# Attention into an expert layer on one core: v kept on partitions 32 to 95, halo rows copied on chip, second buffers for raw k and q, and a new order list

## The chip, the cores and the metric

One core of a Trainium2 chip runs the whole kernel. The metric is the device time of one execution in microseconds (us); the median of several runs is compared. The engines are named as the profile names them: PE (TensorE matmuls), PEld (its weight loads), DVE (VectorE), ACT (ScalarE), POOL (GpSimd) and SP (SyncE). In this kernel POOL issues every load, and SP issues the stores.

## The reference

B = 4 batches, H = 8 heads, S = 768 rows, D = 64. Each query attends to the keys within 15 rows of it and to 24 summaries, one for each block of 32 keys (the maximum of k over the block, the mean of v). The result goes through an expert layer.

```python
k_sum = k.reshape(B, H, nb, 32, D).max(axis=3)
v_sum = v.reshape(B, H, nb, 32, D).mean(axis=3)
scores_l = where(abs(i - j) < 16, scale * q @ k.T, -1e9)
scores_s = scale * einsum('bhsd,bhnd->bhsn', q, k_sum) + log(32)
a = softmax(concatenate([scores_l, scores_s], -1))
x = (a @ concatenate([v, v_sum], 2)).transpose(0, 2, 1, 3).reshape(3072, 512)
h = x @ w_in                               # [512, 2048]
out = (h * clip(h + 3, 0, 6) / 6) @ w_out  # [2048, 512], float32
```

## The kernel before

**Tiles.** A batch has 12 tiles of 64 queries. A tile's keys are a window of 96 rows plus the 24 summaries, 120 in all (`KEYS`). Scores are computed with the keys on the partitions, so that one exponential serves 120 partitions, and `kaug` (k, transposed) and `vaug` hold, for each tile, its 96 window rows and the 24 summaries. The queries are shifted by 16 rows (`PAD`) against the keys, so that a window is 64 rows of its own plus 32 rows that belong to the next tile. In `vaug` the tile's own 64 rows lie on partitions 0 to 63, the 32 rows ahead on 64 to 95, the summaries on 96 to 119. `vaug` has two buffers; batch b uses b % 2.

**Loads.** `load_v` (L381) brings v, a pair of heads at a time, to partitions 0 to 63. The rows ahead come once more from HBM with `load_vhalo` (L388: one POOL DMA at L393, and a small SP DMA at L395) for batches 1 to 3, and are copied on chip by `halo` (L398) for batch 0. Batch 0's k and q are loaded in natural form and transposed by PE (`k_step` L440, `q_step` L482); those of batches 1 to 3 come "raw" (`load_raw` L362: k in four DMAs of 32 partitions, q in eight DMAs of 16 partitions) and are transposed in blocks of 32 by DVE (`turn` L584, with L588, L592 and the maxima of L605). The raw buffers `kraw` and `qraw` are single, so batch 2's raw loads wait for batch 1's transposes. `load_w` (L414) and `load_w2` (L420) bring the expert's weights in four chunks each.

**Work.** `scores` (L502) makes scores (L519), exponential (L527, ACT) and mask (L531, DVE) for a pair of heads and half a batch. `vsum_first` (L546) and `vsum` (L560) make the block means of v with an indicator matrix `ind` and spread them to the tiles. `values` (L613) multiplies with `vaug`, and `finish` normalises, transposes and leaves `x`. The expert layer runs over eight sub-batches of 384 rows: `f1` (L692) is the first product (L700: four matmuls into an `h` bank, the relu at L705 on ACT, the product `g` at L707 on DVE), `f2` (L711) the second: four chunks of four matmuls (L720), a copy out of the bank to `ot` (helper L432), a store. PSUM has two pairs of banks for S, three banks for h, and a single bank, o, for the second product, so a new group of L720 begins when the last one's copy is done.

**Order.** Every operation has a key, and the list `ORDER` names all of them in the order in which they are issued; `Plan.run` (L147) walks it. Each engine executes its own operations in that order. A tag is a letter and numbers: K, Q, V are loads (`K23` is group 3 of batch 2's k), H the halo loads, I and O the chunks of w_in and w_out, k and q the transposes of batch 0, w a `turn`, s scores, u block means, h a halo copy, v values, F and G the expert's first and second product (sub-batch, then group); `.0`, `.1` ... are the steps, and `:A` or `:D` puts a step on ACT or DVE. The planner's costs (`SLOW`, `KRAW`, `LAT`) only decide how many idle matmuls `keep` (L800) puts into PE's early pauses. Waits between engines are put in by the framework from what each operation reads and writes; nothing overtakes on an engine.

Of the kernel before, what the change touches and what calls it, by code (L numbers as in the profile page):

```python
# [15 lines left out]
D = 64  # L16
BLK = 32
# [4 lines left out]
VW = 66  # L22
# [7 lines left out]
c.0 K00.0 c.7 K01.0 c.10 c.11 c.12 c.13 c.9 c.1 Q000.0 K02.0 Q010.0 c.2 c.3 k00.0 k01.0 q010.0 k01.1 k01.4 k00.1 q010.1:A  # L30
k00.4 c.4 k00.3:A k01.2 s010.0 q030.0 q000.0 q000.1:A s030.0 s010.1 s010.2 q020.0 q020.1:A k00.2 q030.1:D k01.3:D k03.0
k03.1 k02.0 k02.1 V00.0 V01.0 c.6 V02.0 V03.0 I0.0 I1.0 Q001.0 s000.0 u00.0 s000.1 u01.0 k03.3:A k03.2 k02.2 u00.1:D u00.2:D
k03.4 u01.1:D s000.2 u01.2:A u00.3:D k02.4 h21.0:D k02.3:D u02.0 s020.0 s030.1 s020.1 s020.2 u03.0 h30.0:D h00.0:D h10.0:D
h01.0:D v00.0 v02.0 u03.1:D u03.2:D v00.2 u01.3:D v00.3 u02.1:A s030.2 h20.0:A u02.2:A Q011.0 I2.0 I3.0 O0.0 O1.0 O2.0 O3.0
K10.0 K11.0 K13.0 K12.0 v01.0 v01.2 v02.1 v00.1 v02.4 v00.4 v00.5 v02.2 v02.3 v02.5 v00.6 v01.1 v01.3 v01.4 v01.5 h31.0:A
v00.7:A u03.3:A q001.0 q011.0 q001.1:A q021.0 q021.1:A u02.3:D q011.1:D v01.6 v02.6 q031.0 s021.0 v01.7:A h11.0:D v02.7:D
c.5 c.8 s021.1 F00.0 F00.1 F00.2 F00.10 F00.3 F01.0 F01.1 s001.0 s001.1 s021.2 q031.1:D F00.4 F01.2 s001.2 F00.11 F00.12
s011.0 F00.13 F00.14 Q121.0 Q101.0 Q110.0 Q100.0 Q120.0 Q131.0 Q130.0 Q111.0 s011.1 s011.2 s031.0 F00.5 F00.6 F00.7 F01.9
F00.8 F00.9 F02.6 s031.1 F01.3 F02.7 F01.10 F01.4 s031.2 F02.8 v04.0 v03.0 F01.6 F01.11 F01.5 v03.1 v03.2 F01.7 F01.8 v04.1
F02.3 F02.4 F02.5 F02.9 v03.3 v03.4:A F02.10 v04.2 F00.15 F02.0 v05.0 v04.3 F00.16 F02.1 F02.11 F00.17 F02.2 v05.1 v05.2  # L40
F03.3 F03.9 F03.0 v04.4:A F03.4 v05.3 F03.1 F03.10 v05.4:A G01.0 F03.5 F03.11 F03.2 F03.6 F10.0 F03.7 F12.0 F03.8 F10.1
F10.3 F12.1 F10.2 F12.2 F10.6 F10.4 F10.9 F10.5 F10.7 F10.8 F11.0 F10.10 F10.11 F11.6 F11.1 F11.9 F11.2 F11.7 F11.8 F11.10
F11.11 F12.6 F12.7 F12.8 F12.9 F12.10 F12.11 w12.0 G01.1 F13.0 F13.1 w13.0 F13.2 w11.0 w13.3 w10.0 w12.3 G01.2 G01.3 F12.3
F13.9 G01.4:A G02.0 G02.1 G02.2 G02.3 F11.3 F13.10 w11.2:A F12.4 F12.5 G02.4:A w12.2:A F13.3 F11.4 F13.4 w10.2:A w13.2:A
w12.4 w11.3 w11.4 w11.1 w11.5:D G00.0 G00.1 s110.0 s110.1 s110.3 w12.1 w13.1 w12.5:D w13.5:A G00.2 G00.3 s120.0 s120.1
s120.3 w13.4 w10.1 F13.5 w10.3 F11.5 w10.4 w10.5:D F13.11 V10.0 V13.0 V11.0 V23.0 V12.0 H1.0 K20.0 K22.0 V20.0 K21.0 Q231.0
K23.0 Q220.0 V22.0 V21.0 Q200.0 Q221.0 Q201.0 Q211.0 Q210.0 Q230.0 s130.0 G00.4:A F13.6 G12.0 s130.3 s130.1 F13.7 G00.5
G01.5 H1.1 G02.5 s120.2 s110.2 s130.2 s100.0 s100.1 F13.8 s100.2 s110.4 s100.3 G12.1 u1.0 u1.1:A u1.3:A u1.5:A G12.2 G12.3
G12.4:A u1.4:D u1.2:D v10.0 s120.4 v10.1 v10.5 v10.6 v10.2 s100.4 u1.7:A u1.6:A u1.9:A G11.0 G11.1 v12.0 v10.3 v10.4:A
u1.8:A v12.1 v12.2 s130.4 G11.2 v10.7 v12.3 v10.8:D G11.3 v12.4:A v13.0 F20.0 F20.3 G11.4:A F20.1 F20.4 v13.5 v13.1 v13.2  # L50
v13.6 F20.9 v13.3 v15.0 F20.10 F20.2 F20.5 F20.11 v15.1 v15.2 F20.6 F21.0 F20.7 F20.8 F21.1 V30.0 V31.0 V32.0 V33.0 F21.2
w21.0 F21.6 G10.0 F21.7 v13.4:A F21.8 F21.3 v15.3 v13.7 F21.9 F22.3 F21.4 F21.5 w20.0 F22.0 G10.1 F21.10 F22.4 v15.4:A
F21.11 F22.1 F22.5 F22.9 F23.0 F22.2 w20.3 F22.10 F22.11 F23.1 w21.2:A v13.8:A F23.2 w22.0 F22.6 u2.0 F22.7 F22.8 w21.3
G10.2 F30.0 F23.6 G10.3 w22.2:A F30.1 w20.4 F30.2 F30.3 F23.3 G10.4:A w22.3 w22.4 G22.0 G22.1 w20.1 u2.1:A w20.2:A F23.7
F23.4 w20.5:A F30.4 G12.5 u2.3 u2.5 G11.5 u2.4 u2.2 F23.5 F23.8 w22.1 s200.0 s200.1 s200.3 F30.5 w22.5:A F31.6 F23.9 G22.2
w23.1 F23.10 F31.7 s220.0 F23.11 F31.8 w21.4 w21.1 w21.5:D F30.9 G22.3 F31.0 F31.3 s220.3 s220.1 s210.0 G22.4:A H2.0 Q301.0
Q330.0 w23.0 K32.0 Q311.0 H3.0 F31.1 w23.5:A Q310.0 Q300.0 Q320.0 Q331.0 F31.2 F31.4 s200.4 F30.10 F30.11 F31.5 G20.0 G20.1
F30.6 F32.3 F33.0 Q321.0 K33.0 K31.0 K30.0 s210.1 s210.3 w23.3 F30.7 w23.4 s200.2 F30.8 w23.2:A F32.4 F33.1 u3.0 u3.1:D
s220.2 F33.2 s220.4 s210.2 G20.2 s230.0 s230.1 s230.3 s230.2 F32.5 G20.3 F31.9 F32.9 F31.10 F31.11 G20.4:A H2.1 G10.5 u3.3
u3.5 H3.1 G20.5 G22.5 v20.0 v20.1 v20.5 v20.2 v20.6 F33.9 G32.0 F32.10 F33.10 v22.0 F33.3 v20.3 F33.11 F32.0 G32.1 F33.4  # L60
v20.4:A v20.7 F32.1 v20.8:A v22.1 v22.2 F33.5 s230.4 F32.2 s210.4 v22.3 F32.11 v22.4:A F33.6 F32.6 F33.7 F32.7 v23.0 F33.8
v23.1 F32.8 F40.0 F40.1 F41.3 G32.2 F40.9 G32.3 F40.10 F41.4 v23.2 F40.2 F40.11 F41.5 v23.5 v23.6 F42.3 F41.9 F42.4 F42.5
F43.0 v25.0 F41.10 G32.4:A v23.3 F41.11 F42.0 F40.6 G30.0 G30.1 v23.4:A F43.1 F42.1 F40.7 v25.1 w30.1 F42.2 F43.2 F40.8
F41.0 F41.1 F41.2 v25.2 F40.3 F40.4 w30.5:A w33.1 w32.1 F42.6 G30.2 G30.3 F42.9 G30.4:A F42.7 v23.7 v23.8:A F42.10 G21.0
G21.1 G21.2 F40.5 w31.0 F42.8 F42.11 F43.3 F43.4 w30.0 w30.3 F43.6 w30.4 F43.5 w31.3 G21.3 F43.7 w32.5:D G21.4:A G21.5 v25.3
F41.6 G31.0 F43.9 G31.1 G31.2 w31.4 F43.8 v25.4:A F41.7 w30.2:A w33.0 F43.10 w31.2:A F41.8 w31.1 w31.5:D w32.0 F43.11 s300.0
F50.9 G31.3 F50.0 s300.1 s300.3 G31.4:A s310.0 s310.3 F50.1 s310.1 G31.5 u3.2 u3.4 G32.5 G30.5 w33.2:A w32.2:D w33.3 w32.3
w33.5:D F50.2 G40.0 F53.0 F53.1 F50.10 w32.4 w33.4 F50.11 G40.1 G40.2 G40.3 G40.4:A s320.0 s320.1 s320.3 F51.0 F53.3 G42.0
F53.4 s330.0 F51.1 s330.3 s330.1 s310.2 s310.4 F53.2 F53.5 s320.2 s300.2 s330.2 F51.2 G42.1 G42.2 F51.6 F51.7 F51.8 F52.3
v30.0 v30.5 v30.1 v30.6 v30.2 F52.0 F52.1 F52.4 F50.3 v32.0 v32.1 F52.2 F52.5 G42.3 G42.4:A F50.4 v30.3 F52.9 s330.4 G41.0  # L70
F51.3 G41.1 F52.10 v30.4:A v32.2 v32.3 v30.7 F51.4 F50.5 s320.4 F52.11 F51.9 v30.8:A F51.10 F51.5 v32.4:A F50.6 F50.7 F51.11
F50.8 s300.4 F52.6 G41.2 F52.7 F52.8 G41.3 F60.0 F60.1 G41.4:D F60.3 v33.0 F60.4 F60.2 F53.9 F53.10 F53.6 F53.7 F53.8 v33.1
F53.11 F60.5 v33.5 v33.6 G50.0 G50.1 v33.2 G41.5 F62.3 G50.2 F61.9 F61.10 G50.3 F62.4 G50.4:A G42.5 F61.11 v33.3 F62.9 v35.0
G51.0 F60.9 F60.10 v33.4:D F62.5 v35.1 v35.2 v35.3 F62.10 v35.4:A F60.11 v33.7 F60.6 G51.1 G51.2 F60.7 F60.8 F62.11 G51.3
G51.4:D v33.8:A F61.3 F61.0 F61.6 F61.4 F61.1 F61.7 F61.2 F61.5 F61.8 G52.0 F63.3 F70.0 G52.1 F72.6 G52.2 F63.4 F70.1 F70.2
F63.5 F73.0 F63.9 F72.7 F73.1 F63.10 F72.8 F73.2 F63.11 G52.3 G51.5 G50.5 G40.5 F63.0 F62.0 F62.6 F62.1 G52.4:D F62.7 F62.2
G62.0 F62.8 F63.6 F63.1 F63.7 F63.2 G62.1 G62.2 F70.9 F70.6 F63.8 G62.3 F70.10 F70.7 F70.11 G62.4:D F70.3 F71.3 F71.4 F70.8
F71.5 G61.0 G61.1 F72.9 F72.10 F70.4 F72.11 F71.6 F71.7 F70.5 F71.8 G61.2 F73.3 F73.4 F73.5 G61.3 F72.3 F71.0 F71.9 G61.4:D
F71.1 F72.4 F71.2 F72.5 F71.10 F71.11 G60.0 F72.0 F73.6 G60.1 G60.2 G72.0 F73.7 F72.1 F72.2 G62.5 G61.5 G52.5 F73.8 F73.9
F73.10 F73.11 G72.1 G71.0 G71.2 G60.3 G72.2 G71.4 G71.6 G70.0 G60.4:A G71.7:A G71.1 G70.1 G71.8 G60.5 G71.3 G71.5 G71.9  # L80
G70.2 G70.3 G70.4:A G71.10:A G71.11 G70.5 G72.3 G72.4:D G72.5
"""

BANKS = ("S", "h", "o")


SLOW = 8.5
TURN = 0.11
LATER = 19.0
KRAW = 2.0  # L90
LAT = {"PE": 0.16, "ACT": 0.08, "DVE": 0.07}


# [15 lines left out]
class Plan:  # L109
# [37 lines left out]
    def run(self):  # L147
# [7 lines left out]
        for token in ORDER.split():  # L155
            key, _, e = token.partition(":")
            o = named.pop(key)
            if e:
                o.eng = {"A": "ACT", "D": "DVE"}[e]
                o.cost, o.lat, o.fn = o.cost[o.eng], LAT[o.eng], partial(o.fn, o.eng)  # L160
# [17 lines left out]
            if o.dma and e == "SP":  # L178
                o.end += o.dma + 1.8 + 0.5 * min(max(line - o.end, 0.0), 4.0)
            elif o.dma:  # L180
                line = max(line, o.end + 1.5) + 1.06 * o.dma
                o.end = line + 0.9
            for b in o.bufs:
# [3 lines left out]
                if b.left == 0:  # L187
                    self.pools[b.pool].append((b.end, b.slot))
                    self.lives.append((b.begin, b.end, b.slot))
            order.append(o)  # L190
        assert not named
        return order


def mm(n, cols):
# [654 lines left out]
```

## Time and profile before

| what | us |
|---|---|
| runs: lowest, median, highest | 234.47, 234.51, 235.97 |
| profiled execution, its own time | 233.64 |
| its span | 231.9 |
| PE busy | 217.3 (94%) |
| DVE busy | 156.7 (68%) |
| ACT busy | 126.5 (55%) |
| POOL busy (it issues the loads) | 72.8 (31%) |
| L700, first product on PE, 536 matmuls | 95.0 |
| L720, second product on PE, 336 + 64 matmuls | 82.3 + 10.9 |
| L527, exponentials on ACT, 32 | 24.8 |

22.14 MB go through the DMA queues, 14.81 MB of it in the 117,280 packets of POOL's queue. The mean granted clock of TensorE is 0.988. The span is what the trace covers; the time of a run also holds what lies around it, 1.74 us here. A row of a group gives line, engine, operation, output and input, the number of instructions, their busy time, the mean of one in ns, and the idle time just ahead of them.

### The profile page before, as it was taken

How to read it: one execution, taken by the hardware profiler on the slowest of the kernel's cores; microseconds unless marked ns; L12 is line 12 of the kernel's file. 1: busy time of each engine (PE TensorE's matmuls, PEld its weight loads, DVE VectorE, ACT ScalarE, POOL GpSimd, SP SyncE). 2: the span in 40 equal slices, each digit the busy share in tenths (PEclk: the TensorE clock that was granted, in tenths of full speed). 3: DMA queues.
4: the chain of work that ended last, by engine and by line, in shares of the span. 5: the costliest groups of instructions: out<-in, count | busy, mean ns of one | idle time of the engine just before them, and what ended most of it. 6: DMA issues, size and time to landing. Idle time of an engine off the chain costs nothing.

```text
span 231.9 us, 5321 instructions
## 1 busy us (share of the span) xinstructions
PE 217.3 (94%) x2175; PEld 121.8 (52%) x2175; DVE 156.7 (68%) x327; ACT 126.5 (55%) x258; POOL 72.8 (31%) x86
## 2 busy tenths in 40 slices
PE   7899699999989997989999889999999999999991
PEld 2365476555445563545565445555555555555560
DVE  2489689789897669889785499945955645454201
ACT  2287567774588854768654535675552543434101
POOL 7994481357754734707741200000000000000000
PEclk9999979999999999999999999999999999999998
DMA  5999999999999999999999990132002030012013
GB/s 76 169 123 182 191 206 196 119 77 87 95 120 176 186 103 86 85 114 146 84 142 89 127 71 0 45 80 84 3 11 85 0 136 3 0 45 90 3 68 114
DMA packets 126585, 22.14 MB, mean 95 GB/s; under 512 B 116960, under 2 KB 123616, under 8 KB 126560
## 3 DMA queue, kind: packets, MB, share of 16 engines
q0 software_dynamic: 117280, 14.81, 217.7%
q1 hardware_dynamic: 9280, 6.98, 12.7%
q8 instruction: 17, 0.28, 0.7%
q14 instruction: 8, 0.07, 0.1%
HBM read 29.60 MB, written 6.29 MB: 155 GB/s over the span
## 4 chain that ended last, share of the span: by engine, by line
PE 58%; DMA 18%; issue 9%; POOL 9%; ACT 2%; DVE 2%; DVEq 0%; POOLq 0%
PE h L700 26%; PE o L720 22%; DMA kraw<-in_k_dram 13%; DMA qnat<-in_q_dram 5%; PE h L720 4%; POOL vaug L385 3%; ACT at L527 2%; PE S L519 1%; PE S L632 1%; POOL qraw L375 1%; POOL qnat L357 1%; PE S L682 1%; POOL knat L346 1%; POOL win L417 1%; POOL kraw L367 1%
## 5 line engine op out<-in xcount | busy, mean ns | idle before, releaser
L700 PE MATMUL h<-x,win 128*128 128x384 bf16 (+1 forms) x536 | 95.0, 321 | 3.1 <-DVE g L707 3.1
L705 ACT ACTIVATE r<-h 128x384 f32<-128x384 f32 x128 | 60.4, 493 | 59.4 <-PE h L700 58.7
L707 DVE SCALAR_TENSOR_TENSOR g<-r,h 128x384 bf16<-128x384 f32 x128 | 67.5, 545 | 33.9 <-ACT r L705 32.1
L720 PE MATMUL o<-wout,g 128*128 128x512 bf16 x336 | 82.3, 379 | 0.2 <-ACT ot L432 0.2
L700 PEld LDWEIGHTS <-win 128*128 128x128 bf16 x536 | 49.9, 99 | 37.5 <-issue 3.6
L720 PEld LDWEIGHTS <-g 128*128 128x128 bf16 x400 | 38.1, 98 | 36.3
L375 POOL DMA_DIRECT2D qraw<-in_q_dram x24 | 21.3, 890 | 29.1 <-issue 10.5
L527 ACT ACTIVATE at<-S 120x768 bf16<-120x768 f32 x32 | 24.8, 812 | 7.1 <-PE S L519 7.1
L367 POOL DMA_DIRECT2D kraw<-in_k_dram x12 | 15.8, 1317 | 13.5 <-issue 12.0
L385 POOL DMA_DIRECT2D vaug<-in_v_dram x16 | 15.1, 949 | 4.8 <-PE h L700 3.1
L592 DVE STREAM_TRANSPOSE qaug<-qraw 128x800 bf16<-128x800 bf16 x12 | 11.8, 998 | 6.2 <-DMA kraw<-in_k_dram 3.3
L667 DVE TENSOR_TENSOR xn<-S,rc 128x512 bf16<-128x512 f32 (+1 forms) x25 | 15.7, 643 | 0.4
L531 DVE TENSOR_TENSOR at<-at,mask 96x768 bf16<-96x768 bf16 x28 | 14.8, 546 | 1.5 <-ACT at L527 1.0
L432 ACT COPY ot<-o 128x512 f32<-128x512 f32 x16 | 9.4, 586 | 11.3 <-PE o L720 10.6
L588 DVE STREAM_TRANSPOSE kaug<-kraw 128x768 bf16<-128x768 bf16 x12 | 11.5, 965 | 2.1 <-DMA kraw<-in_k_dram 2.1
L432 ACT COPY x<-S 128x512 bf16<-128x512 bf16 x19 | 11.0, 587 | 2.5 <-PE S L682 2.1
L519 PEld LDWEIGHTS <-kaug 64*128 64x128 bf16 x384 | 7.0, 96 | 8.2 <-issue 6.3
L605 DVE TENSOR_REDUCE red<-kaug 128x24 bf16<-128x768 bf16 x12 | 11.2, 940 | 0.0
L519 PE MATMUL S<-qaug,kaug 64*128 64x64 bf16 x384 | 9.2, 192 | 2.0 <-ACT at L527 1.2
L803 PE MATMUL o<-idle 128*128 128x512 bf16 x30 | 9.5, 442 | 1.5 <-DVE idle L287 1.5
L720 PE MATMUL h<-wout,g 128*128 128x512 bf16 (+1 forms) x64 | 10.9, 326 | 0.0
L632 PEld LDWEIGHTS <-at 120*64 120x64 bf16 x384 | 7.6, 111 | 5.9 <-issue 4.8
(84 smaller groups left out, 139.3 us busy)
## 6 DMA issues: line engine op xcount, KB each, us to landing
out_dram<-ot SPq DMA_DIRECT2D x19, 256.0 KB
vaug<-in_v_dram POOLq DMA_DIRECT2D x16, 192.0 KB, 10.7
kraw<-in_k_dram POOLq DMA_DIRECT2D x12, 192.0 KB, 14.8
qraw<-in_q_dram POOLq DMA_DIRECT2D x24, 96.0 KB, 11.9
win<-in_moe_w_in_dram POOLq DMA_DIRECT2D x4, 512.0 KB, 11.8
wout<-in_moe_w_out_dram POOLq DMA_DIRECT2D x4, 512.0 KB, 13.5
vaug<-in_v_dram POOLq DMA_DIRECT2D x3, 380.0 KB, 16.2
out_dram<-ot SPq DMA_DIRECT2D x4, 224.0 KB
```

The costliest lines, as they stand in the source:

```text
L367: op("POOL", 0.8, lambda hs=hs, ds=ds, rows=rows: nc.gpsimd.dma_start(out=kraw[rows], in_=k[b, hs].rearrange("h (c r) d -> r (h c) d", r=B ...
L375: nc.gpsimd.dma_start(out=qraw[lo:lo + PAD, 1 - x:1 - x + NP * NB], in_=src[PAD * (1 - x):PAD * (2 - x)])
L385: op("POOL", 0.95, lambda: nc.gpsimd.dma_start(out=o[0:QB, lo:hi, 0:D], in_=rows[:, lo:hi]), w=[("v", b % 2, c)], prio=prio, dma=1.7)
L432: {"ACT": nc.scalar.copy, "DVE": nc.vector.tensor_copy, "POOL": nc.gpsimd.tensor_copy}[eng](o, i)
L519: nc.tensor.matmul(X[p, half].slot[:, j, i * QB:(i + 1) * QB], kaug[p][rows, t], qT[rows, p, t * QB:(t + 1) * QB], start=not masked, stop= ...
L527: op("ACT", act(2 * HALF), lambda a=a, x=x: nc.scalar.activation(a, x.slot[0:KEYS, :, 0:HALF], AF.Exp, scale=scl), r=[x], w=[("at", p, hal ...
L531: op("DVE", dve(2 * HALF, 1.92), lambda m=m, half=half: nc.vector.tensor_tensor(m, m, mask[:, half * HQ:(half + 1) * HQ].unsqueeze(1).to_b ...
L667: nc.vector.tensor_tensor(o, src[..., 0:D], r.unsqueeze(len(r.shape)).to_broadcast(list(o.shape)), op=ALU.mult)
L700: nc.tensor.matmul(h.slot[:, lo * 128:hi * 128], w_in_sb[:, kt, ft * 128:(ft + 1) * 128], xt[s].slot[:, kt, lo * 128:hi * 128], start=(kt ...
L705: op("ACT", act(HALF), lambda: nc.scalar.activation(r.slot[:], h.slot[:, 0:HALF], AF.Relu, bias=0.5, scale=1.0 / 6.0), r=[h], w=[r], prio= ...
L707: op("DVE", dve(HALF), lambda: nc.vector.scalar_tensor_tensor(gt[s].slot[:, ft], r.slot[:], 1.0, h.slot[:, 0:HALF], op0=ALU.min, op1=ALU.m ...
L720: nc.tensor.matmul(o.slot[:, a:z], gt[s].slot[:, ft, ts * 128:(ts + 1) * 128], w_out_sb[:, ft, a:z], start=(ft == 0), stop=(ft == NFT - 1))
```

## The change

- `VW`, the row length of `vaug`, goes from 66 to 80.
- v is loaded to partitions 32 to 95. The window of a tile is now its own 64 rows and the 32 rows before it, on partitions 0 to 31, and queries are shifted the other way. Tile 0 takes its 32 rows from tile 11 (masked where they don't count).
- `load_vhalo` is gone. `halo` copies partitions 64 to 95 of a tile to partitions 0 to 31 of the next, for every batch (24 copies more; 14 stand on ACT, 10 on DVE in the list).
- `ind` has 96 rows, and block means are taken over partitions 0 to 95, so `vaug`'s first 32 partitions are cleared before (`empty`): buffer 0 on DVE, buffer 1 on POOL.
- Half 0 of a batch is now tiles 6 to 11 (`low`).
- `kraw` and `qraw` have two buffers each; the second ones share memory with batch 0's natural k and q. Raw q comes in one DMA of 32 partitions per group (12 issues for 24), and `turn` transposes 768 columns of q for 800.
- The second half of batch 0's q comes in 128-row pieces (`load_wide`, four DMAs), transposed by 12 matmuls (`q_rest`) for 32.
- Values of batch 0's first half, heads 4 to 7: the summaries are multiplied in matmuls of their own, 24 rows from a compact tile `vf`, not spread to tiles first.
- `ORDER` is rewritten, sorted by planned begin before issue (an engine's own order stays); `SLOW`, `KRAW` and the counts of idle matmuls change. In the last sub-batch the group split into two half-width pieces is another one and comes last.

```diff
-VW = 66
+VW = 80
-SLOW = 8.5
+SLOW = 4.5
-KRAW = 2.0
+KRAW = 1.6
...
+        order.sort(key=lambda o: o.begin)
...
-    kraw = sb([128, NP * NB, BLK], BF16, "kraw")
-    qraw = sb([128, NP * NB + 1, BLK], BF16, "qraw")
+    first = sb([128, 2 * NP * NB, BLK], BF16, "first")
+    kraw, qraw = ([sb([128, NP * NB, BLK], BF16, f"{n}raw"), first[:, i * NP * NB:(i + 1) * NP * NB]] for i, n in enumerate("kq"))
...
-    ind = sb([QB, NQ, 32], BF16, "ind")
+    ind = sb([WIN, NQ, 32], BF16, "ind")
...
+        def empty(eng, i, c):
+            eng.memset(vaug[i][0:BLK, 2 * c:2 * c + 2, :, 0:D].bitcast(F32), 0.0)
+            if i == 0:
+                eng.memset(vf[c][WIN:KEYS, :, D:D + 2], float(BLK))
+        for c in range(NP):
+            plan.at(f"z{c}")
+            op("DVE", 0.95, lambda c=c: empty(nc.vector, 0, c), r=["idle"], w=[("vz", 0, c), ("vf", c)], prio=-100 + c)
+            op("POOL", 1.0, lambda c=c: empty(nc.gpsimd, 1, c), w=[("vz", 1, c)], prio=-29.95 + 0.01 * c)
...
-        op("POOL", 0.95, lambda: nc.gpsimd.dma_start(out=o[0:QB, lo:hi, 0:D], in_=rows[:, lo:hi]),
+        op("POOL", 0.95, lambda: nc.gpsimd.dma_start(out=o[BLK:WIN, lo:hi, 0:D], in_=rows[:, lo:hi]),
...
-        op("POOL", 0.75, lambda: nc.gpsimd.dma_start(out=o[QB:WIN, 0:n - 1, 0:D], in_=rows[0:WIN - QB, 1:n]),
-        op("SP", 0.7, lambda: nc.sync.dma_start(out=end[QB:WIN, :, NQ - 1, 0:D], in_=end[0:WIN - QB, :, 0, 0:D]),
...
+    def halo(b, c, x, prio):
+            copy(eng, o[0:BLK, hs, a:z, 0:D], o[QB:WIN, hs, a - 1:z - 1, 0:D])
+            if x:
+                copy(eng, o[0:BLK, hs, 0, 0:D], o[QB:WIN, hs, NQ - 1, 0:D])
+        op(EITHER, {"ACT": 0.75 + 0.1 * x, "DVE": 0.42 + 0.1 * x}, go, r=[("v", i, c), ("vz", i, c)], w=[("vh", i, c, x)], prio=prio,
...
-            op("DVE", dve(BLK + S), lambda: nc.vector.transpose(
+            op("DVE", dve(S), lambda: nc.vector.transpose(
```

The part of the new list around the end of batch 0 (z1.1, z3.1 and z2.1 are clears of the second `vaug` buffer, on POOL):

```
V13.0 V10.0 V11.0 Q11.0 Q13.0 Q12.0 Q10.0 V20.0 K20.0 K22.0 K23.0 z1.1 z3.1 z2.1 V21.0 V22.0 K21.0 h120.0:A h121.0:A F12.5 Q23.0 z0.1
V23.0 Q20.0 Q22.0 Q21.0 G02.2 G02.3 F12.9 F11.9 G02.4:A w11.0 w11.2:A G00.0 G00.1 G00.2 G00.3 w12.0 w13.0 w10.0 F12.10
```

Ahead of it, behind the last w_out chunk, stand K13, K10, K12, V12 and K11.

## The prediction

> **What bounds the kernel now.** I read the page's table of the span in 40 slices first, then what TensorE waited for, then DMA rates by stage, and last GpSimd's queue in order of time.
>
> The slices (5.8 us each): TensorE, its granted clock, the DMA engines.
>
> ```profile
> PE   7899699999989997989999889999999999999991
> PEclk9999979999999999999999999999999999999998
> DMA  5999999999999999999999990132002030012013
> ```
>
> TensorE is full from slice 7 on; DMA is full to slice 25 and nearly idle behind it. So bytes can matter before about 140 us only, and behind that the time is TensorE's work. TensorE's waits (in all, times, longest):
>
> ```profile
> PE h L700 <- DVE g L707: 3.1, 2, 1.7
> PE S L493 <- DMA qnat<-in_q_dram: 1.6, 1, 1.6
> ...
> PE S L519 <- ACT at L527: 1.2, 3, 0.7
> ...
> PE S L519 <- DVE qaug L592: 0.8, 1, 0.8
> ```
>
> Little is left to win: 3.1 us for g (at 88.6 and 134.1), 0.8 for the transposed q (at 100.6), and 1.6 at the opening for the second half of q, which ends at 27.21. The first matmul of the expert's first product (L700) stands at 30.30, the first of sub-batch 2 ("F20", the first work that needs batch 1's attention) at 79.81, the last matmul ends at 227.29.
>
> Rates, in windows of 1 us (columns: stretch, length, busy time and instructions of PE, PEld, DVE, ACT, POOL, granted clock, DMA share, GB/s):
>
> ```profile
> 30.00:31.00 1.00, 1.00 (x19) 0.91 (x16) 1.00 (x2) 0.59 (x1) 1.00 (x1) 0.50 1.23 205
> 41.00:42.00 1.00, 1.00 (x24) 0.66 (x22) 0.91 (x2) 0.90 (x3) 0.40 (x1) 1.00 4.37 112
> 44.00:45.00 1.00, 1.00 (x10) 0.53 (x8) 0.23 (x2) 0.94 (x3) 0.00 (x0) 1.00 4.40 119
> 52.00:53.00 1.00, 1.00 (x7) 0.49 (x5) 0.78 (x3) 0.72 (x2) 0.81 (x1) 1.00 7.61 80
> 64.00:65.00 1.00, 1.00 (x6) 0.47 (x5) 1.00 (x4) 1.00 (x2) 0.94 (x1) 1.00 4.65 119
> ```
>
> Weights on 128 partitions: 205. At 41.4 the last w_out is in. Raw k on 32 partitions then runs at 119, raw q on 16 rows at 80, v on 64 partitions (at 64) at 119. A load of 196,608 B at 119 takes 1.65 us.
>
> GpSimd's queue (start, length, instruction, idle before and its releaser):
>
> ```profile
> 19.56 0.81 POOL L417 DMA_DIRECT2D win<-in_moe_w_in_dram  x1 [1.26 <-DMA vaug<-in_v_dram]
> ...
> 63.63 1.31 POOL L367 DMA_DIRECT2D kraw<-in_k_dram  x1 [1.19 <-issue]
> 65.28 0.95 POOL L385 DMA_DIRECT2D vaug<-in_v_dram  x1 [0.34 <-issue]
> 68.69 1.31 POOL L367 DMA_DIRECT2D kraw<-in_k_dram  x1 [2.46 <-issue]
> ```
>
> Two limits show. The weight load at 19.56 waits for a v load that it has nothing to do with: the DMA issued eight before it. Rows at 21.43, 24.21 and 27.19 do the same, so a DMA waits until the eighth before it has landed. The pauses "issue" between 61 and 73 name no releaser; they fit a limit of about 16,384 outstanding packets (v 1,536, raw k 3,072): before 63.63, 13,792 + 3,072 exceeds it until a v lands, and the 5.06 us from 63.63 to 68.69 are three v's, 1.69 each. That is my inference.
>
> **The change, part by part.** What decides is one placement. The new first 32 partitions of the second v buffer are cleared on GpSimd, pair by pair. The new list puts three of these clears (pairs 1, 3, 2) behind the issue of the raw k load K23 of batch 2. ScalarE's next instructions are the two copies of batch 1's rows for pair 2 (h120, h121), which need pair 2's clear; behind them on ScalarE stands G02.4, the copy that empties the only "o" bank; and TensorE's next but a few is G00.0, which needs that bank. So TensorE stops until K23 is issued, three clears are made and three ScalarE copies are done.
>
> When is K23 issued? The eighth DMA before it is V11. Up to the last w_out the bytes are the same, save that batch 0's four v loads sit on partitions 32 to 95. No row has that shape: at 205 it would be 0.96 us, at 119 1.65. I take 1.2, nearer the natural k and q loads on 96 partitions, which run at 150 to 190. That saves 4 × 0.47 = 1.9: the last w_out lands at 41.4 − 1.9 = 39.5. Then four raw k at 1.69 and four v at 1.2: V11 lands at 39.5 + 6.8 + 4.8 = 51.1. Raw q in one load of 32 rows has raw k's shape, so 1.69 instead of two halves (98,304 B at 80: 1.23 each). Bounds for a raw load: 1.65, and 2.56, the mean of batch 1's eight (41.4 to the last landing at 61.88).
>
> By packets, K23 would make four q, one v, three k = 23,040 outstanding; three q's must land first: 51.1 + 5.1 = 56.2. Its issue takes 1.31: 57.5.
>
> A clear: 32 × 768 four-byte elements. The memsets of 384 and 128 elements take 0.437 and 0.223 on GpSimd, 0.00084 us per element, so 0.223 + 640 × 0.00084 = 0.76 each; bounds 0.44 (no dearer than 384) and 1.52 (if four-byte elements count twice). Three: 2.3, to 59.8. The ScalarE copies: rows 0.831, then 0.722 + 0.291, to 61.6; the bank's copy 0.586, to 62.2; TensorE goes on at 62.3.
>
> When would TensorE have been there? Batch 0's first values end at 25.27 now, 1.9 earlier with the faster v, and the second q no longer holds TensorE to 27.21, as 128-wide pieces follow the third w_in chunk: first L700 at about 23.5. Up to G00.0 the list has 27 product groups of 0.65, four chunks of 0.863, some 4 of batch 0's second half, and 1.5 of waits: about 50. **The stall is some 12 us.** At 30 the clock is 0.50 after idle from 25.6 to 27.2, and that spell (28.3 to 31.9) loses 1.7; I charge 1.7 once.
>
> From 62.2: ScalarE's list up to batch 1's first exponential is four copies and spreads of k and v (mean 0.7), eight spreads at 0.828, six small ones: 13.2, to 75.4. Four rounds of scores, two exponentials of 0.81 each, with the listed work between: 8.4, to 83.8. Then five chunks (4.3), the values and transposes of six tiles (16 matmuls 0.41 and four transposes 0.35 each: 4.6), waits 1.9: F20 at 94.6, against 79.81.
>
> From F20 to TensorE's end before: 147.5. Take off the stalls that the second raw buffers and the list remove (1.37 + 0.79 + 1.73 = 3.9), and work that now lies ahead of F20: one chunk (0.86), one tile's values and transposes (0.76), two tiles' transposes (0.70) = 2.3. TensorE ends at 94.6 + 141.3 = 235.9. The tail was 4.6; the last copy is half as wide (0.376 on ScalarE for 0.69) and has one store issued for three: 3.9. Span 239.8 + 1.7 for the clock = 241.5. Before's profiled run was 233.64 for 231.9 (+1.74), the median 0.87 above that run: 241.5 + 2.6 = **244**.
>
> Edits priced at nothing: the three halo loads (issue 1.33, some 3.2 us of DMA each) and their store-queue moves leave a queue that is no longer the bound once TensorE is 10 us late; without that cover they are a gain. The 24 new row copies (14 ScalarE, 10 VectorE, 0.4 to 1.0 each) beyond the first two lie in idle time: ScalarE is busy 55%, VectorE 68%. Twenty-four more small matmuls: 16 take 0.41, so 0.6, ahead of the stall, which absorbs it. The same holds for twelve 128-wide transposes in place of 32, the idle matmuls, and VectorE's clears of the first buffer. The wider row stride (80 for 66) is in no row; the 32x768 copies (0.411 VectorE, 0.831 ScalarE) could move either way; I take zero, bounds −0.1 and +0.1 on each of three copies on the path.
>
> A rule that bears on the v load: the Trainium skill, "SBUF — State Buffer", section "Door 1: The DMA port swizzle", says partitions 0 to 63 reach only 8 of 16 ports, as 0 to 31 do, while crossing partition 64 switches to the others. The equal 119 on 32 and 64 partitions and 205 on 128 agree; by it v would take 0.96, and the sum would be about 1.9 lower.
>
> **Rivals.**
> *B, only the eight-deep wait holds.* The packet limit is inferred, and before 35 us POOL issued four raw k in a row. Then K23 starts at 51.1 and everything is 5.1 earlier: 239. For it: "issue" names nothing. Against: the 63.63 to 68.69 pauses.
> *C, faster.* The clears are done before TensorE asks for the bank; this decides at about 50 us. It needs V11 in by 45, that is eight loads in 5.5 us, or K23 not waiting on it. Then batch 1's last q lands at 57.9 (51.1 + 4 × 1.69), F20 follows 17.9 behind, as before (61.88 to 79.81), plus 2.3 and four ScalarE copies (3.4): 81.5; 81.5 + 141.3 + 3.9 + 2.6 = 229. The rates speak against it; the shorter queue and 3.9 us of removed stalls for it.
> *D, v does not load faster there* (the change doesn't do what it says): eight v's at 1.65, 3.6 later: 248. Raw loads at 2.56 would add 7 × 0.87 = 6.1: 250. The even 119 in 41 to 46 speaks against the latter.
>
> **How the numbers follow.** A 0.50 (244), B 0.22 (239), D and slow raw loads 0.10 (248 to 250), C 0.12 (229), something between C and B 0.06. About 1% (2.3 us) is what a measurement of this kernel tells from no change. The range leaves out C and the far end of D: 236 to 250; clears at 0.44 or 1.52 each (−1.0, +2.3) and v at 0.96 or 1.65 lie in it. Faster by over 1% (below 232.2): 0.13. Within: 0.06. Slower: 0.81.
>
> **What would show it.** A wait of L720 on ScalarE's copy of ot of about 12 us ending near 62; GpSimd's memsets near 58 to 60, behind a raw k load that pauses on "issue"; the clock at half behind it; v loads near 160 GB/s; no wait for g at L700 over 1 us. It is wrong if the memsets are done before 50, or if TensorE's first batch-1 scores are before 70.

## The result

The changed kernel takes 246.54 us (median of four, 245.66 to 247.57), the kernel before 235.09 beside it; the ratio is 1.049, 95% interval 1.042 to 1.055. It is slower by some 11.5 us, 2.5 us above the forecast time. The profiled execution was 245.66, its span 244.0.

The same three rows of the page's 40 slices (6.1 us each now):

```profile
PE   7999899960298599999999999999999999999994
PEclk9999999995599779999999999999999999999999
DMA  5999999999999800999920030004031001112022
```

TensorE has a hole in slices 9 to 11, and the clock is at half in 10 and 11 and lower once more in slices 14 and 15. From slice 16 on both are full to the end. DMA has a hole of its own in slices 15 and 16: batch 2's loads are done and batch 3's not yet issued. The list of TensorE's waits (us in all, times, longest) names the hole:

```profile
PE o L748 <- ACT ot L443: 13.3, 3, 12.9
PE S L537 <- ACT at L546: 3.3, 4, 1.8
...
PE h L728 <- DVE g L735: 1.1, 2, 0.6
PE S L537 <- DVE qT L613: 0.5, 1, 0.5
```

The first row is L720 of before under its new number: the second product waits for ScalarE to empty the single o bank. The waits for g and for the transposed q, 3.1 and 0.8 before, are 1.1 and 0.5. The chain of work that ended last (start, length, what) says where ScalarE was:

```profile
53.98 2.10 issue
56.08 1.32 POOL first L393
57.40 0.50 issue
57.90 1.31 POOL first L393
59.21 0.51 issue
59.72 0.11 POOL first L393
...
61.02 2.12 POOL vaug L342 x3
...
63.90 0.92 ACT vaug L443 x2
64.81 0.49 ACT ot L443
...
65.34 1.01 PE o L748 x2
```

Read from below: TensorE goes on when the bank is empty, the bank is emptied behind two row copies (`vaug` L443), these wait for three clears on GpSimd (L342), and the clears stand behind three raw k loads of batch 2 (`first`, the second raw buffer), each of which pauses on "issue".

### The profile page after: what moved, and what is told of

It is laid out like the page before. It is cut to its first block, busy times and chain, and to the rows that moved or that the text cites. A ratio compares the mean times of both kernels' runs of the same rounds, so it can differ in the third digit from the quotient of the medians.

```text
span 244.0 us, 5330 instructions
## 1 busy us (share of the span) xinstructions
PE 218.7 (90%) x2165; PEld 121.8 (50%) x2165; DVE 162.0 (66%) x341; ACT 140.2 (57%) x286; POOL 65.1 (27%) x75
## 4 chain that ended last, share of the span: by engine, by line
PE 81%; ACT 7%; DVE 4%; POOL 3%; issue 3%; DVEq 0%; POOLq 0%; ACTq 0%
PE h L728 33%; PE o L748 28%; PE h L748 4%; ACT vaug L443 3%; PE o L831 3%; PE S L657 3%; PE S L537 3%; PE S L710 2%; ACT at L546 1%; DVE g L735 1%; POOL first L393 1%; PE h L459 1%; PE S L588 1%; ACT r L733 1%; DVE vaug L443 1%
## 5 line engine op out<-in xcount | busy, mean ns | idle before, releaser
L728 PE MATMUL h<-x,win 128*128 128x384 bf16 (+1 forms) x536 | 95.8, 322 | 1.2 <-DVE g L735 1.1
L748 PE MATMUL o<-wout,g 128*128 128x512 bf16 x336 | 84.2, 387 | 13.3 <-ACT ot L443 13.3
L728 PEld LDWEIGHTS <-win 128*128 128x128 bf16 x536 | 49.7, 98 | 36.4 <-issue 2.8
L748 PEld LDWEIGHTS <-g 128*128 128x128 bf16 x400 | 38.6, 99 | 51.3 <-issue 16.6
L443 ACT COPY vaug<-vaug 32x640 bf16<-32x640 bf16 (+2 forms) x24 | 12.9, 586 | 14.9 <-POOL vaug L342 14.3
L695 DVE TENSOR_TENSOR xn<-S,rc 128x512 bf16<-128x512 f32 (+1 forms) x25 | 15.8, 643 | 0.5
L443 ACT COPY ot<-o 128x512 f32<-128x512 f32 x17 | 9.9, 585 | 6.7 <-PE o L748 5.6
L537 PE MATMUL S<-qT,kaug 64*128 64x64 bf16 x384 | 9.7, 196 | 4.1 <-ACT at L546 3.3
L443 ACT COPY x<-S 128x512 bf16<-128x512 bf16 x19 | 11.0, 588 | 3.6 <-PE S L710 1.7
L393 POOL DMA_DIRECT2D qraw<-in_q_dram x8 | 10.5, 1311 | 3.1 <-issue 3.0
L393 POOL DMA_DIRECT2D kraw<-in_k_dram x8 | 10.6, 1328 | 2.7 <-DMA wout<-in_moe_w_out_dram 1.8
L443 DVE COPY vaug<-vaug 32x768 bf16<-32x768 bf16 (+2 forms) x24 | 7.0, 317 | 5.2 <-issue 2.6
L443 ACT COPY kaug<-h 128x576 bf16<-128x576 bf16 (+3 forms) x16 | 5.6, 419 | 6.8 <-PE h L459 5.8
## 6 DMA issues: line engine op xcount, KB each, us to landing
wout<-in_moe_w_out_dram POOLq DMA_DIRECT2D x4, 512.0 KB, 12.9
```

The source lines that it names most:

```text
L393: op("POOL", 1.32, lambda src=src, o=o, hs=hs, ds=ds, rows=rows: nc.gpsimd.dma_start(out=o[rows], in_=src[b, hs].rearrange("h (c r) d -> r ...
L443: {"ACT": nc.scalar.copy, "DVE": nc.vector.tensor_copy, "POOL": nc.gpsimd.tensor_copy}[eng](o, i)
L537: nc.tensor.matmul(X[p, half].slot[:, j, i * QB:(i + 1) * QB], kaug[p][rows, t], qT[rows, p, t * QB:(t + 1) * QB], start=not masked, stop= ...
L695: nc.vector.tensor_tensor(o, src[..., 0:D], r.unsqueeze(len(r.shape)).to_broadcast(list(o.shape)), op=ALU.mult)
L728: nc.tensor.matmul(h.slot[:, lo * 128:hi * 128], w_in_sb[:, kt, ft * 128:(ft + 1) * 128], xt[s].slot[:, kt, lo * 128:hi * 128], start=(kt ...
L748: nc.tensor.matmul(o.slot[:, a:z], gt[s].slot[:, ft, ts * 128:(ts + 1) * 128], w_out_sb[:, ft, a:z], start=(ft == 0), stop=(ft == NFT - 1))
```

## The experiments

Theory 1: the place of the clears in GpSimd's order makes the loss. Its rivals: the loads of batch 1 are late anyway; the single o bank is the cause; other parts of the change cost time.

**Clears early.** The whole edit, in the list:

```diff
-K23.0 z1.1 z3.1 z2.1 V21.0 V22.0 K21.0 h120.0:A h121.0:A F12.5 Q23.0 z0.1
+K23.0 V21.0 V22.0 K21.0 h120.0:A h121.0:A F12.5 Q23.0
-... c.9 h021.0:A k03.3:A K13.0
+... c.9 h021.0:A k03.3:A z2.1 z1.1 z3.1 z0.1 K13.0
```

> The four clears of the second v buffer are issued on GpSimd ahead of batch 1's first raw k load instead of behind K23; nothing else is moved. Theory 1 (the place of the clears makes the stall): TensorE's wait for the o bank's copy (12.9 us, ending at 65.3) is gone, ScalarE's wait for the clears too, the clock does not fall to half at 55 to 69, the clears take 2.9 us near 27 to 31 and delay nothing, since the loads behind them wait for landings anyway. Then the wait of 12.9 and some 1.7 of slow clock go, and batch 1's scores start when the last raw q of batch 1 is transposed: 231 to 234. Rival (the stall only shows what the loads would cost anyway: raw k and q of batch 1 land too late): a wait of 8 us or more comes back ahead of batch 1's scores, 241 to 246.

Measured: 230.72 (230.46 to 231.35), ratio to the kernel before 0.982 (0.976 to 0.988). The time lies just under the 231 to 234 that was expected. The clears took their time where it costs nothing (GpSimd in order of time):

```profile
25.49 1.48 POOL L434 DMA_DIRECT2D wout<-in_moe_w_out_dram  x2 [1.80 <-DMA win<-in_moe_w_in_dram]
26.95 2.80 POOL L342 MEMSET vaug<- 32x768 f32 x4
29.67 3.97 POOL L393 DMA_DIRECT2D kraw<-in_k_dram  x3
```

The first raw k behind them is issued at 29.67 for 27.10 in the changed kernel, and lands no later: 12.7 us after its issue for 15.8, so at 42.4 for 42.9. TensorE's waits are

```profile
PE S L537 <- ACT at L546: 3.6, 4, 2.4
...
PE o L748 <- ACT ot L443: 0.4, 2, 0.2
```

The wait of 12.9 is gone and nothing of its size has come back; 15.8 us less for moving four memsets. It is faster than both kernels. Against the expectation the clock does still fall, for a shorter time (last section).

**Clears between.** All four clears behind V20 and ahead of K20, three raw loads earlier than in the change.

```diff
-V20.0 K20.0 K22.0 K23.0 z1.1 z3.1 z2.1
+V20.0 z1.1 z3.1 z2.1 z0.1 K20.0 K22.0 K23.0
```

> The four clears are issued between V20 and K20, so three raw k loads earlier than in the changed kernel (three clears ended at 63.1 there; V20 was issued at 53.04 to 53.98). Theory 1 is a matter of dose: three clears end at 54.0 + 2.1 = 56.1, so 7.0 us earlier than 63.1, TensorE's wait is 12.9 - 7.0 = 5.9, the time falls by 7 and by up to 1.7 if the clock stays up: 238 to 240. Rival (ScalarE's row copies or batch 1's raw loads end last whatever the clears do): less than 3 us gained, above 243.5.

Measured: 238.87, ratio 1.017 (1.011 to 1.023). The clears start at 53.89, right behind V20, and the wait is 6.1:

```profile
52.96 0.94 POOL L404 DMA_DIRECT2D vaug<-in_v_dram  x1
53.89 2.79 POOL L342 MEMSET vaug<- 32x768 f32 x4
56.61 2.63 POOL L393 DMA_DIRECT2D first<-in_k_dram  x2
```

```profile
PE o L748 <- ACT ot L443: 6.5, 3, 6.1
```

The clears begin 7.1 us earlier and the time falls by 7.7: the dose that theory 1 asks for. Three of the clears were moved ahead of three DMA issues, the fourth ahead of four more; nothing else was changed.

**The bank emptied first.** G02.4 ahead of the row copies on ScalarE, the clears left behind K23.

```diff
-K21.0 h120.0:A h121.0:A F12.5 ... F12.9 F11.9 G02.4:A w11.0
+K21.0 F12.5 ... F12.9 F11.9 G02.4:A h120.0:A h121.0:A w11.0
```

> The clears stay behind K23; ScalarE empties the o bank (G02.4) before the two row copies that wait for the clears. Theory 1a (the bank only hands on the wait: everything ScalarE has behind the row copies, and the block sums of batch 1 on TensorE, need the clears anyway): TensorE gets through the second product's G00 (3.5 us) and then stands about 9 us or more in front of batch 1's block sums or their copies; the first exponential of batch 1 moves by less than 2 us; 243 to 247. Rival (the single bank is the cause, and the order of three ScalarE copies would be cure enough): the wait is gone, 232 to 237.

Measured: 245.87, ratio 1.046 (1.040 to 1.053). TensorE's longest wait is now

```profile
PE S L588 <- ACT vaug L443: 13.8, 1, 13.8
```

The wait has moved from the bank to batch 1's block means (L588), which read the rows that ScalarE's copies fill. It lasts until the copies behind the fourth clear are done (69.13 to 70.05), and the first exponential comes at 81.17 for 79.94. The bank only handed the wait on; the rival falls.

**Loads alone.** Weights, raw k and v are loaded, with attention and the expert layer left out; one tile of zeros is stored. Weights stand ahead, then eight raw k, then v in four ways, each behind a weight chunk.

```python
def values(b, dst, lo):                 # v of batch b to partitions lo to lo + 63
    o, rows = dst[:].rearrange("p h t d -> p (h t) d"), v[b].rearrange("h (t r) d -> r (h t) d", r=QB)
    for c in range(4):
        a, z = 2 * c * NQ, 2 * (c + 1) * NQ
        nc.gpsimd.dma_start(out=o[lo:lo + QB, a:z, 0:D], in_=rows[:, a:z])
```

> Loads alone, no attention and no expert layer (one tile of zeros is stored): four weight chunks, eight raw k loads, then four times a weight chunk and four v loads: to partitions 32 to 95 with a row stride of 80, to 0 to 63 with 80, to 32 to 95 with 66, to 0 to 63 with 66. Packets: if a limit of 16,384 outstanding packets holds, a raw k load pauses on issue before the eighth-before rule can stop it (the sixth or seventh k, 1 to 2 us); if only the eight-deep rule holds, the k loads up to the eighth are issued without a pause. Placement: if partitions 32 to 95 load faster, those eight v loads run at 150 GB/s or more and the eight on 0 to 63 at about 120; if not, all at about 120. Stride: 66 and 80 within 5% of each other; if the stride mattered, 80 differs from 66 on both places.

GpSimd in order of time:

```profile
1.24 3.14 POOL L75 DMA_DIRECT2D wout<-in_moe_w_out_dram  x4 [0.80 <-PEq L115]
4.33 5.29 POOL L65 DMA_DIRECT2D kraw<-in_k_dram  x4
13.45 1.32 POOL L65 DMA_DIRECT2D kraw<-in_k_dram  x1 [3.83 <-issue]
18.06 1.31 POOL L65 DMA_DIRECT2D kraw<-in_k_dram  x1 [3.29 <-issue]
19.93 1.31 POOL L65 DMA_DIRECT2D kraw<-in_k_dram  x1 [0.56 <-issue]
```

The fifth raw k is the ninth DMA. The eighth before it, the first weight chunk, had landed at 7.6 (issued at 1.24, the shortest time to landing 6.4); the load was issued at 13.45. The eight-deep rule cannot hold it there. Packets can: the queue's 53,760 packets less eight raw k of 3,072 and sixteen v of 1,536 leave 576 for a weight chunk; with two chunks and five raw k out it would be 16,512, with one 15,936, so a limit of 16,384 holds the load until the third chunk is in; that chunk landed at 13.1 (issued at 2.87, 10.2 to landing). The pause came a load earlier and lasted about twice as long as expected, but of the two readings only the packet limit allows one. That the limit is exactly 16,384 isn't shown.

As for the place of v: the eight loads to 32 to 95 ran at 156 GB/s, the four to 0 to 63 with stride 80 at 156 too, and those to 0 to 63 with 66 at 156 at first and near 120 from 56.5 on. Being last, that group could have been slow for want of neighbours, so the order was turned round.

**Loads alone, another order.**

```diff
-    high80, low80, high66, low66, a weight chunk ahead of each
+    low66, low80, high66, high80, a weight chunk ahead of each; then all four again without; then weights
```

> Loads alone as before, in another order: after the weights and raw k, v to 0 to 63 with stride 66, to 0 to 63 with 80, to 32 to 95 with 66, to 32 to 95 with 80, four loads each behind a weight chunk; then the same sixteen loads without weights between; then two weight chunks. In the first run of loads alone, v ran at 156 GB/s on both places and both strides, save the last three, 0 to 63 with 66, at about 120. Theory S66 (stride 66 on 0 to 63 is the slow one): it runs at about 120 again, now as the first group, and the others at 156. Theory M (loads with nothing else behind them in the queue are slow): all four groups at 156 while weights stand between, 120 only in a group whose neighbours are v loads.

One window out of each of the first four groups (length, DVE and POOL busy, clock, DMA share, GB/s):

```profile
36.00:37.00 1.00, 0.00 (x0) 0.37 (x2) 1.00 4.88 119
43.00:44.00 1.00, 0.00 (x0) 0.48 (x2) 1.00 2.45 157
50.00:51.00 1.00, 0.00 (x0) 0.94 (x1) 1.00 2.44 155
58.00:59.00 1.00, 0.00 (x0) 0.68 (x2) 1.00 2.45 156
```

Again 0 to 63 with a stride of 66 is slow, now as the first group; the other three are not. But in the second pass without weights, 156 lasts to 63, 118 to 131 follow from 64 to 74, and 145 to 155 from there on. The slow stretch is longer than four loads of one kind can take. By their landings, the eight loads to 0 to 63 of that pass, with 66 and then with 80, came in 1.7 us apart (62.7 to 76.7), the eight to 32 to 95 behind them 1.2 (76.7 to 86.2). Over both runs, groups on 0 to 63 were slow four times in six, groups on 32 to 95 never in six. So place seems to play a part, but neither place nor stride is the cause by itself: on 0 to 63 a stride of 80 was fast behind a weight chunk and slow without. What it is stays open.

**Stride 66 in the kernel with early clears** (`VW = 66`, nothing else).

> The kernel with early clears, and v's row length 66 again instead of 80, everything else left. Theory S (the stride sets the rate of v loads: in the profiles they ran at 97 to 117 GB/s with 66 on partitions 0 to 63, and at 146 to 156 with 80 on 32 to 95): batch 0's v loads at 12 to 16 us fall to about 115, first product 1.5 to 2 us later, 232 to 234. Theory P (the partitions set it) or M (neither, but what stands behind them in the queue): the rate stays near 150 and the time within 0.7 us of 230.7.

Measured: 230.86 (0.986, 0.978 to 0.994); the windows from 12 to 15 show 149 to 152 GB/s, the first L728 stands at 24.35. On 32 to 95 the stride is worth nothing that shows.

**One buffer for raw k and q again**, with early clears, batch 2's and 3's raw loads put behind the transposes.

```diff
-            in_=kraw[(b + 1) % 2][:, p * NB:(p + 1) * NB]...
+            in_=kraw[0][:, p * NB:(p + 1) * NB]...
```

> The kernel with early clears, but one buffer each for raw k and raw q again; batch 2's and 3's raw loads are issued behind the transposes that free them. If the second buffers remove before's waits for g and for the transposed q (1.37 + 0.79 + 1.73 us), as the prediction said: these waits come back, 3 to 5 us more than 230.7. Rival (the list and the row copies on chip, that is the three halo loads less, removed them): less than 1 us more, since batch 2's raw loads still land by about 90, and its scores begin near 89.

Measured: 232.55, 0.993 (0.989 to 0.997), beside 230.86 for the run before it on the same chip: some 1.7 us, between both expectations, with intervals that overlap. That the second buffers are worth something is likely, not shown. The 3 to 5 us of the first expectation did not come, so the 3.9 us that the prediction put on them and the list together are not the buffers' alone; which wait makes up the difference wasn't read.

**Batch 1's spreads by DMA**, with early clears: eight ScalarE copies go to the store queue (`if b > 1` becomes `if b > 0` in `vsum`, and the list loses the eight steps).

> The kernel with early clears, and the eight spreads of batch 1's block means (0.83 us each on ScalarE, 57 to 65.5) done by DMAs of the store queue as in batches 2 and 3. If ScalarE's queue is what holds batch 1's first exponential (at 65.49, with TensorE idle 2.4 us and the clock at half to 72 behind it): the wait shrinks to under 1 us, the clock stays up, 227 to 229. Rival (batch 1's last q transposes, which end at 68.9, hold the scores anyway, or the 16 small DMAs stand in the full queue and batch 1's values wait): within 1 us of 230.7 or above.

Measured: 229.76, 0.984 (0.973 to 0.996), not to be told from early clears. It lies within 1 us of 230.7, as the rival said. The first exponential moved from 65.49 to 63.58, and TensorE's waits between the score rounds went over to VectorE: 2.1 us for the transposed q (L613) and 1.2 for the exponentials, which had been 3.6 with early clears.

**A warm clock through the stall**: the change as it is, and 56 idle matmuls ahead of G00.0.

> The changed kernel with its clears behind K23, and 56 idle matmuls on TensorE (0.22 us each) ahead of G00.0, where it stands for 12.9 us; they write to a free S bank that nothing reads. The prediction charged 1.7 us for the half clock behind the stall. If that time is on the path: the clock stays at 1.00, G00's sixteen matmuls take 3.5 instead of 5.1 us, the time falls by 1.2 to 2, to 244.5 to 245.3. Rival (ScalarE's 14.6 us of listed work from the clears to batch 1's first exponential end last, and TensorE's slow stretch lies beside them): the clock stays up, the first exponential stays within 0.4 us of 79.9, the time within 0.7 us of 246.5.

Measured: 246.09 (244.17 to 246.63), against 246.54: within the spread of either, as the rival said. TensorE took 3.6 us for G00's sixteen matmuls in place of 5.1, and the first exponential came at 78.93 for 79.94, which is more than the 0.4 that the rival allowed. Behind it TensorE waited 2.4 us between score rounds, and the clock was at 0.50 from 80 to 84; in the changed kernel it was so from 82 to 88 (slices 14 and 15). So the half clock behind the stall itself cost about 1 us on the way to the first exponential, and a cost of 1.7 isn't shown.

**Early clears again, and with the pauses filled**, side by side on one chip. The second adds the spreads by DMA and moves G10.1, F13.6 and G10.2 in between the score rounds.

> The kernel with early clears once more, so that it stands beside the next one on the same chip: ratio to the kernel before 0.976 to 0.988.

> Early clears, batch 1's spreads by DMA, and three pieces of TensorE work (two chunks of G10 and one group of F13, 2.4 us) moved in between batch 1's four score rounds, where TensorE waited 3 to 4 us for exponentials and transposes and the clock fell to half until 72. If these pauses are what is left to win: pauses between the rounds under 1 us in all, no half clock, 2 to 4 us less than the early clears alone. Rival (the S banks, which the exponentials free, set the pace of the rounds and of batch 1's values behind them): the pause comes back ahead of the values, less than 1 us gained.

Measured: early clears 231.13, 0.992 (0.988 to 0.995), above the expected band; filled 230.94, 0.986 (0.981 to 0.991). Less than 1 us between the medians: the rival holds as far as the time goes; whether the pause came back where it said wasn't read. On two chips early clears are thus 0.8% and 1.8% faster than the kernel before, not more.

## Why the prediction was right

The mechanism was the one named, link by link, and the time lies in the range. The sizes, step by step:

| step | forecast | measured |
|---|---|---|
| first L700 (now L728) | 23.5 | 24.33 |
| TensorE stops | 50 | 52.47 |
| K23 issued | 56.2 | 59.72 |
| three clears | 2.3 | 2.1 |
| TensorE goes on | 62.3 | 65.34 |
| its stall | 12 | 12.87 |
| first exponential of batch 1 | 75.4 | 79.94 |
| F20 | 94.6 | 99.78 |
| F20 to TensorE's end | 141.3 | 140.7 |
| tail | 3.9 | 3.5 |
| span | 241.5 | 244.0 |

- **The one mis-sized term** is the landing of batch 1's loads. Their issue and time to landing (here the last w_out chunk, V11, and the third raw q, issued at 26.37, 44.20 and 50.44) give 41.2, 54.2 and 59.4:

```profile
wout<-in_moe_w_out_dram POOLq DMA_DIRECT2D x1, 512.0 KB, 14.8
vaug<-in_v_dram POOLq DMA_DIRECT2D x1, 192.0 KB, 10.0
qraw<-in_q_dram POOLq DMA_DIRECT2D x1, 192.0 KB, 9.0
```

  The sum had 39.5 for w_out and 51.1 for V11. The start was 1.7 late; the eight loads up to V11 took 13.0 for 11.6, raw k 1.9 and v 1.4 each (1.69 and 1.2 in the sum); the three q's took 5.2 for 5.1, and K23 was issued 0.3 behind the third. That is the 3.5 us of K23. In the start lies a wrong reading: in the kernel before the last w_out landed not at 41.4 but at 42.8 (issued at 27.92, 14.9 to landing).
- **A second miss of 1.1 us**: the fourth clear (z0.1) stands behind K21 and Q23, and ScalarE waited for it once more at 68.33. The sum looked at three clears only. TensorE went on 3.0 late; with this 1.1 and another 1.0 on the way, whose cause isn't shown, F20 came 5.2 late. The span is only 2.5 late: the stretch behind F20 and the tail took 0.6 and 0.4 less, and the 1.7 charged apart for the clock covered the rest. No run shows these 1.7 as a cost of their own, so that part of the agreement is luck.
- **The removed stalls** are borne out: the three waits behind F20 (1.37, 0.79 and 1.73) are gone, and no wait of TensorE stands behind 99.78 in the changed kernel.
- **The packet limit** (forecast against rival B) is borne out: K20, K22 and K23 start at 56.08, 57.90 and 59.72, each 0.3 behind the landing of one raw q. With that q still out, each would have made 16,896 outstanding packets, without it 13,824. The loads alone pause where the eight-deep rule lets them go. B would have had K23 start when V11 had landed, at 54.2.
- **Rival C** gave 229 if the clears are made in time. That is early clears, 230.7 and 231.1.
- **Rival D** fell in the kernel: v ran at 146 to 150 GB/s in the windows from 13 to 15 (1.2 us a load was taken; 196,608 B at 150 is 1.3). But the place alone doesn't make it: in loads alone, 0 to 63 with a stride of 80 was as fast behind a weight chunk. The Trainium skill, "SBUF — State Buffer", section "Door 1: The DMA port swizzle", puts the rate down to the ports that the partitions reach, 8 for 0 to 63 and more for 32 to 95; 156 GB/s on both speaks against that as the limit in those groups; what slows 0 to 63 in others is open.
- **The edits priced at nothing** weren't separated: with the clears early, the whole of the change is a gain of 3 to 5 us, in which the removed stalls are counted too.

## What to carry to other kernels

Here three clears of 2.1 us in all cost a stall of 12.9 because they were put behind DMA issues: on a queue that issues transfers, a memset waits for landings that have nothing to do with it. Three issues earlier the stall was 6.1, ahead of all of them it was gone. Follow such a step from its engine's queue to the first instruction that reads it, and from there to what stands behind that reader on its own engine. Where a list is written by hand, look first for compute steps between DMA issues that can go ahead of them.

## What the runs showed of the hardware

- GpSimd's DMA issue stopped for something besides the count of eight: 3.83 us at the ninth DMA, when the eighth before it had landed 5.8 us earlier. A limit near 16,384 outstanding packets fits this pause and those of K20, K22 and K23; it is an estimate from these counts.
- The same v load ran at 156 or near 120 GB/s. 0 to 63 with a stride of 66 was slow as first and as last group, the other three shapes fast when weights stood between; without weights 0 to 63 was slow with both strides, 32 to 95 with neither. The reason is open.
- A short idle is enough for the clock. In the kernel with early clears TensorE idled from 63.96 to 66.35, and the clock was at half behind it:

```profile
64.00:66.00 2.00, 0.00 (x0) 0.09 (x1) 1.63 (x3) 1.96 (x3) 1.34 (x2) 0.99 2.58 171
66.00:68.00 2.00, 1.01 (x24) 0.73 (x24) 1.60 (x4) 1.98 (x5) 1.29 (x1) 0.50 2.30 216
```

The Trainium skill, "TensorE: Matmul & The Clock Gate", section "HAM oscillation — how this bites in real kernels", gives idle gaps of more than about 3.4 us as what lets the clock fall; here 2.4 us did. In the kernel before, the 1.6 us from 25.6 to 27.2 were followed by the half clock too (from 28.5, after a further wait of 0.4), while 1.73 us (132.4 to 134.1) left it at 1.00. So the length of one idle stretch doesn't decide it alone.
